# An attention block in decode: scores of one pair placed ahead of the value products of the pair in front of it

## The chip, the cores and the metric

The kernel runs on one core of one Trainium2 chip. The metric is the time of one execution on the device in microseconds (us), and for a kernel the median of several such runs. One further execution is recorded by the hardware profiler; from it come the profile and the trace. The engines are PE (matrix products), PEld (its weight loads), DVE (vector), ACT (scalar and activation functions), POOL and SP (SyncE, which here issues all the loads). L12 is line 12 of the kernel.

## The reference, cut to what matters

```python
# x: 2 rows (batch b) of 512; 32 query heads, 8 key/value heads of 128; the last W = 4096 positions
mod = silu(c) @ w_mod                                  # six vectors sa, ca, ga, sb, cb, gb per row
h = layernorm(x) * (1 + ca) + sa
q = h @ wq                                             # 32 heads of 128
scores = q . k_cache[b, head // 4, -4096:] * 128**-0.5
p = softmax(scores)
o = p . v_cache[b, head // 4, -4096:]
x = x + ga * (o @ wo)
h = layernorm(x) * (1 + cb) + sb
x = x + gb * (silu(h @ w1) @ w2)                       # w1 is 512 x 1792, w2 is 1792 x 512
```

Everything is float32. The data are read once: 16 key blocks and 16 value blocks of 2.10 MB each (8 heads, 2 batch rows), and beside them w_mod (6.3 MB), wq and wo (8.4 MB each), w1 and w2 (3.7 MB each), 97.5 MB in all.

## The kernel before, in words

**Loads.** All large loads go through one ring of 8 tiles of 2 MB in SBUF (`ring`, `RING = 8`) and are issued by SP in the order of the program: four of w_mod, four of wq, then keys and values, four of wo (L95), three of w1 and five of w2 (L95). A load waits on SP until the tile that is eight loads back in this order has been read for the last time; every load behind it on SP's queue waits with it. `fetch(t)` (L338) issues the keys of pair t (L79) and the values of pair t-1 (L86).

**Head.** The modulation, the first layer norm and the queries are computed while the first loads run; the queries are laid out block by block in `qbd`.

**The loop over pairs.** A pair is a key head with a batch row; there are 16 (`seq`, `NP`). For one pair t these steps are made:

- `keys(t, 0..3)` (L349): DVE transposes the key tile in four quarters into `kT` (two buffers).
- scores `s` (L425): PE, 16 products, which the trace shows as 32, since each is made in two passes. Then DVE takes the maximum of each row, `mx` (L433).
- row of maxima: PE turns `mx` into a row, `mT` (L368); DVE takes the maximum per query head, `mg` (L371), and spreads it, `mrow` (L377); PE turns it back into a column, `bp` (L385); ACT copies it to `bias` (L387).
- exponentials `pr` (L389) on ACT, with their sum in `rowsum`.
- the probabilities are brought into the layout of weights: DVE transposes to `xp` (L399) and multiplies to `zp` (L401), PE permutes to `pT` (L412), ACT copies to `ptb` (L419).
- `weighted` (L304): PE, 8 value products `o` (16 passes, L311), in two rounds over four column groups, then ACT copies the result to `ob` (L319).
- `collect` (L322): PE adds the four parts into `o_all` (L325), one bank that holds the sums of all pairs.

Iteration t of the loop (L359) makes the keys, scores and maxima of pair t, and everything behind the maxima of pair u = t-1. Nearly all of these instructions go through `inorder = tc.keep_in_program_order`, so each engine takes them in the order in which they are written. So the orders of the engines in iteration t are:

- PE: mT(u), bp(u), pT(u), o(u), s(t), o_all(u)
- DVE: keys 0 of t, mg(u), mrow(u), keys 1 of t, xp(u), zp(u), keys 2 and 3 of t, mx(t)
- ACT: bias(u), pr(u), ptb(u), ob(u)
- SP: keys of pair t+1, values of pair t

**Tail.** The sums are divided by the row sums (`on`, L476), transposed by `oq` (L479) and copied to `oTn` (L482); then the product with wo (`acc_o` L504, `ao` L513), the second layer norm, `hid` with w1 (L545), silu (L562 to L574), and the product with w2 (`acc_yw` L578, `acc_y` L588, `yo` L598). The five loads of w2 use the ring tiles that the last values and the four tiles of wo leave.

Of the kernel before, what the change touches and what calls it, by code (L numbers as in the profile page):

```python
# [8 lines left out]
F32 = mybir.dt.float32  # L9
AF = mybir.ActivationFunctionType  # L10
ALU = mybir.AluOpType
AX = mybir.AxisListType  # L12

P = 128
B, D = 2, 512
HQ, HKV, DH = 32, 8, 128
G = HQ // HKV
# [6 lines left out]
def adaln_block(  # L24
# [21 lines left out]
    nc = tc.nc  # L46
    SK = k_cache.shape[2]
    W = min(4096, max(256, SK // 4))
    SCALE = DH**-0.5
# [4 lines left out]
    id4 = head.tile([P, 32], F32, name="id4")  # L54
# [3 lines left out]
    work = ctx.enter_context(tc.tile_pool(name="work", bufs=2))  # L58
    once = ctx.enter_context(tc.tile_pool(name="once", bufs=1))
# [3 lines left out]
    def const(shape, name):  # L63
        return consts.tile(shape, F32, name=name)

    def bank(tag, name):
        return (psum1 if tag in "CO" else psum).tile([P, 512], F32, tag=tag, name=name)
# [9 lines left out]
    def load_k(b, h):  # L77
        t = stream(f"k{h}_{b}")
        nc.sync.dma_start(  # L79
            t, k_cache[b, h, SK - W :, :].rearrange("(p n) d -> p (n d)", p=P)  # L80
        )
        return t

    def load_v(b, h):
        t = stream(f"v{h}_{b}")
        nc.sync.dma_start(  # L86
            t, v_cache[b, h, SK - W :, :].rearrange("(p n) d -> p (n d)", p=P)
        )
        return t
# [25 lines left out]
    ident = const([P, P], "ident")  # L115
# [20 lines left out]
    group = const([P, 4], "group")  # L136
# [27 lines left out]
    negscale = const([1, 1], "negscale")  # L164
# [3 lines left out]
    mrow = [const([1, P], f"mrow{i}") for i in range(2)]  # L168
    ptb = [const([P, P + 16], f"ptb{i}") for i in range(2)]
# [4 lines left out]
    qbd = [const([P, 4, B, 4, 32], f"qbd{n}") for n in range(2)]  # L174
# [3 lines left out]
    rowsum = const([P, HKV, B], "rowsum")  # L178
# [88 lines left out]
    for k in range(4):  # L267
        wv = wqt[k].rearrange("p (n s g m) -> p n g s m", n=2, s=4, g=G)
        for n in range(2):
            for g in range(G):  # L270
# [4 lines left out]
                    start=(k == 0),  # L275
                    stop=(k == 3),
# [24 lines left out]

    o_all = bank("O", "o_all")[:, : B * DH].rearrange("p (b d) -> p b d", b=B)

    def weighted(t, b, h, vt):  # L304


        pt = ptb[t % 2]
        o_ps = bank("D", f"o{t}")
        for n in range(8):
            c = n % 4  # L310
            inorder(nc.tensor.matmul(  # L311
                o_ps[32 * c : 32 * c + 32, :],
                pt[:, 16 * n : 16 * n + 32],
                vt[:, 512 * n : 512 * n + 512],
                start=(n < 4),
                stop=(n >= 4),
            ))
        o_sb = once.tile([P, 4 * DH], F32, tag="wide", name=f"ob{t}")
        inorder(nc.scalar.copy(o_sb, o_ps))  # L319
        return o_sb  # L320

    def collect(t, b, h, o_sb):  # L322

        for m in range(4):
            inorder(nc.tensor.matmul(  # L325
                o_all[32 * m : 32 * m + 32, b, :],
                selh[:, m, HQ - G - G * h : 2 * HQ - G - G * h],
                o_sb[:, m * DH : (m + 1) * DH],
                start=(t == 0),
                stop=(t == NP - 1),  # L330
                skip_group_check=True,
            ))

    seq = [(h, b) for h in range(HKV) for b in range(B)]
    NP = len(seq)
    kt, vt, wot, kT = {}, {}, [], {}

    def fetch(t):  # L338

        if t < NP:  # L340
            kt[t] = load_k(seq[t][1], seq[t][0])
        if t > 0:
            vt[t - 1] = load_v(seq[t - 1][1], seq[t - 1][0])

    def keys(t, n4):

        if n4 == 0:
            kT[t] = ktp.tile([P, 4, 32, 32], F32, tag="kT", name=f"kT{t}")
        inorder(nc.vector.transpose(  # L349
            kT[t][:, :, 8 * n4 : 8 * n4 + 8, :].rearrange("p j n k -> p n j k"),  # L350
            kt[t][:, n4 * 1024 : (n4 + 1) * 1024].rearrange("p (n j r) -> p n j r", j=4, r=32),
        ))

    inorder = tc.keep_in_program_order
    fetch(0)
    s_ps, mx = {}, {}
    for t in range(NP + 1):  # L359
        last, now = t > 0, t < NP  # L360
        if now:
            fetch(t + 1)
            keys(t, 0)
        if last:
            u = t - 1
            h, b = seq[u]
            mT = bank("B", f"mT{u}")
            inorder(nc.tensor.matmul(mT[0:1, :P], mx[u], ident, start=True, stop=True))  # L368
            m = mrow[u % 2]
            mg = work.tile([1, G], F32, tag="mg", name=f"mg{u}")  # L370
            inorder(nc.vector.tensor_reduce(  # L371
                mg,
                mT[0:1, :P].rearrange("o (c i g) -> o g c i", c=4, g=G)[:, :, :, 0:4],
                axis=AX.XY,
                op=ALU.max,
            ))
            inorder(nc.vector.tensor_copy(  # L377
                m.rearrange("o (c i g) -> o c i g", c=4, g=G)[:, :, 0:4, :],
                mg[:, None, None, :].to_broadcast([1, 4, 4, G]),
            ))  # L380
        if now:
            keys(t, 1)
        if last:
            bp = bank("B", f"bp{u}")
            inorder(nc.tensor.matmul(bp[:, 0:1], m, negscale, start=True, stop=True))  # L385
            bias = work.tile([P, 1], F32, tag="bias", name=f"bias{u}")
            inorder(nc.scalar.copy(bias, bp[:, 0:1]))  # L387
            pr = once.tile([P, 8, 32], F32, tag="pr", name=f"pr{u}")
            inorder(nc.scalar.activation(  # L389
                pr.rearrange("p s k -> p (s k)"),  # L390
                s_ps[u],
                AF.Exp,
                bias=bias,
                scale=SCALE,
                accum_out=rowsum[:, h, b : b + 1],
            ))

            xp = once.tile([P, 8, 32], F32, tag="xp", name=f"xp{u}")
            inorder(nc.vector.transpose(xp, pr))  # L399
            zp = once.tile([P, 4, 8, 16], F32, tag="zp", name=f"zp{u}")  # L400
            inorder(nc.vector.tensor_mul(  # L401
                zp,
                xp[:, None, :, 0:16].to_broadcast([P, 4, 8, 16]),
                group[:, :, None, None].to_broadcast([P, 4, 8, 16]),
            ))
        if now:
            keys(t, 2)
            keys(t, 3)
        if last:
            tp = bank("C", f"pT{u}")[:, :P]  # L410
            for i in range(4):
                inorder(nc.tensor.matmul(  # L412
                    tp[32 * i : 32 * i + 32, :],
                    id4,
                    zp.rearrange("p c s x -> p (c s) x")[:, :, 4 * i : 4 * i + 4],
                    start=True,
                    stop=True,
                ))
            inorder(nc.scalar.copy(ptb[u % 2][:, :P], tp))  # L419
            o_sb = weighted(u, b, h, vt[u])  # L420
        if now:
            s_ps[t] = bank("A", f"s{t}")[:, :256]
            for j in range(4):
                for cc in range(4):
                    inorder(nc.tensor.matmul(  # L425
                        s_ps[t][32 * cc : 32 * cc + 32, :],
                        qbd[seq[t][0] // 4][:, seq[t][0] % 4, seq[t][1], j, :],
                        kT[t][:, j, 8 * cc : 8 * cc + 8, :],
                        start=(j == 0),
                        stop=(j == 3),  # L430
                    ))
            mx[t] = work.tile([P, 1], F32, tag="mx", name=f"mx{t}")
            inorder(nc.vector.tensor_reduce(mx[t], s_ps[t], axis=AX.X, op=ALU.max))  # L433
        if last:
            collect(u, b, h, o_sb)

    gaT, sbT, cbT = turned(ga, "gaT"), turned(sb, "sbT"), turned(cb1, "cbT")
    nc.vector.tensor_copy(hT[:, :, 1:32:16], sbT[:, :, 0:32:16])
# [24 lines left out]
    for b in range(B):  # L463
        for m in range(4):
# [4 lines left out]
                start=True,  # L469
                stop=True,  # L470
# [31 lines left out]
    for q in range(24):  # L502
        g = q % 4
# [4 lines left out]
            start=(q < 4),  # L508
            stop=(q >= 20),
        )  # L510
    for q in range(24, 32):
        for g in range(4):
# [4 lines left out]
                start=(q == 24),  # L517
                stop=(q == 31),
# [24 lines left out]
    for k in range(4):  # L543
        for g in range(4):
# [4 lines left out]
                start=(k == 0),  # L549
                stop=(k == 3),  # L550
# [25 lines left out]
    for tt in range(WIDE):  # L576
        g = tt % 4
# [4 lines left out]
            start=(tt < 4),  # L582
            stop=(tt >= WIDE - 4),
        )
    y = bank("D", "acc_y")[:, :P]
    for tt in range(WIDE, T2):
        for g in range(4):
# [4 lines left out]
                start=(tt == WIDE),  # L592
                stop=(tt == T2 - 1),
# [35 lines left out]
```

## Time and profile before

| | |
|---|---|
| median of 3 runs | 255.24 us (252.54 to 255.28) |
| time of the profiled execution | 254.44 us |
| its span, first to last instruction | 252.7 us |
| mean granted PE clock | 0.797 of full speed |
| PE busy | 153.7 us (61%) |
| DVE busy | 119.3 us (47%) |
| ACT busy | 35.5 us (14%) |
| loads | 97.5 MB, on average 386 GB/s over the span |
| value products o, one pass | 945 ns mean, 256 of them |
| scores s, one pass | 411 ns mean, 512 of them |
| transposes of keys, a quarter | 1224 ns mean, 64 of them |

Busy shares are averages over the head, the loop (46 to 222 us) and the tail. Passes on PE overlap, so their mean durations do not add up to its busy time. In the profile's slices the span is cut into 40 equal parts of 6.3 us; a digit is the busy share of a slice in tenths, and 9 is 90% or more. The chain that ended last is followed back from the last instruction; each of its lines gives the start, the duration and the work, and in time between them an engine takes over from another.

### The profile page before, as it was taken

What the parts mean: (1) busy time and instruction counts of PE and PEld (TensorE: products, weight loads), DVE (VectorE), ACT (ScalarE), POOL (GpSimd) and SP (SyncE); (2) the same over time, 40 slices, a digit from 0 to 9 for tenths busy, and PEclk for the clock granted to TensorE, in tenths of its full rate; (3) what the DMA queues carried; (4) which work ended last, traced back from release to release, by engine and by line L of the source; (5) the groups of instructions that cost most, each with busy time, mean ns of one, the idle gap of its engine ahead of it and who ended that gap; (6) DMA issues with size and microseconds to landing.
All of it is one profiled execution on the core that took longest, in us unless ns stands there. A gap on an engine that the chain in (4) does not pass through costs nothing.

```text
span 252.7 us, 3508 instructions
## 1 busy us (share of the span) xinstructions
PE 153.7 (61%) x1476; PEld 55.6 (22%) x1476; DVE 119.3 (47%) x212; ACT 35.5 (14%) x96; POOL 9.3 (4%) x30
## 2 busy tenths in 40 slices
PE   0294736555484764845749385583754849679754
PEld 0221001121231222212223121221212313232412
DVE  0703004845649457485463837549476490210230
ACT  2200000112211111112111101211012110100320
POOL 9300001000000000000000000000000000000000
PEclk9997597675978979779575977978879786657979
DMA  7999999999999999999999999999999999953800
GB/s 261 428 434 425 436 425 431 440 420 431 433 428 438 418 431 441 420 438 425 431 436 420 438 424 433 431 428 433 429 431 428 427 428 433 398 204 122 293 2 1
DMA packets 7607, 97.75 MB, mean 387 GB/s; under 512 B 920, under 2 KB 936, under 8 KB 1576
## 3 DMA queue, kind: packets, MB, share of 16 engines
q1 hardware_dynamic: 7592, 97.54, 91.5%
q8 instruction: 11, 0.18, 0.3%
q14 instruction: 4, 0.03, 0.0%
HBM read 97.53 MB, written 0.00 MB: 386 GB/s over the span
## 4 chain that ended last, share of the span: by engine, by line
PE 49%; DVE 23%; DMA 15%; ACT 8%; issue 4%; SPq 0%; DVEq 0%; ACTq 0%
PE o L311 20%; PE s L425 13%; DMA wq<-in_A_wq_dram 12%; DVE kT L349 9%; DVE zp L401 4%; PE pT L412 4%; ACT pr L389 4%; DVE xp L399 3%; PE acc_o L504 3%; DVE mx L433 3%; DMA wm<-in_w_mod_dram 2%; PE bp L385 2%; ACT ptb L419 2%; PE q L271 1%; PE acc_yw L578 1%
## 5 line engine op out<-in xcount | busy, mean ns | idle before, releaser
L349 DVE STREAM_TRANSPOSE kT<-k 128x1024 f32<-128x1024 f32 x64 | 77.0, 1224 | 0.0
L311 PE MATMUL o<-v,ptb 128*32 128x512 f32 x256 | 51.3, 945 | 6.0 <-ACT ptb L419 6.0
L425 PE MATMUL s<-kT,qbd 128*32 128x256 f32 x512 | 36.8, 411 | 2.5 <-DVE kT L349 2.3
L433 DVE TENSOR_REDUCE mx<-s 128x1 f32<-128x256 f32 x16 | 6.8, 425 | 62.8 <-PE s L425 62.8
L412 PE MATMUL pT<-zp,id 128*32 128x128 f32 x128 | 10.1, 403 | 33.8 <-DVE zp L401 33.6
L425 PEld LDWEIGHTS s<-kT,qbd 128*32 128x32 f32 x512 | 17.3, 121 | 30.7 <-issue 17.7
L271 PE MATMUL q<-wq,hq_T 128*32 128x512 f32 x64 | 12.8, 943 | 10.0 <-DMA wq<-in_A_wq_dram 10.0
L311 PEld LDWEIGHTS o<-v,ptb 128*32 128x32 f32 x256 | 9.5, 158 | 34.0 <-issue 21.0
L319 ACT COPY ob<-o 128x512 f32<-128x512 f32 x16 | 9.4, 587 | 53.4 <-PE o L311 53.4
L385 PE MATMUL bp<-negscale,mrow 1*128 1x1 f32 x32 | 6.0, 256 | 16.7 <-DVE mrow L377 16.7
L387 ACT COPY bias<-bp 128x1 f32<-128x1 f32 x16 | 2.5, 159 | 63.6 <-PE bp L385 63.6
L401 DVE TENSOR_TENSOR zp<-xp,group 128x512 f32<-128x512 f32 x16 | 11.1, 692 | 0.5
L412 PEld LDWEIGHTS pT<-zp,id 128*32 128x32 f32 x128 | 3.6, 135 | 34.7 <-issue 34.5
L280 DVE STREAM_TRANSPOSE qT<-q 128x512 f32<-128x512 f32 x2 | 1.4, 716 | 20.1 <-PE q L271 20.1
L368 PE MATMUL mT<-ident,mx 128*1 128x128 f32 x32 | 6.1, 271 | 5.6 <-DVE mx L433 5.6
L385 PEld LDWEIGHTS bp<-negscale,mrow 1*128 1x128 f32 x32 | 4.7, 182 | 21.4 <-DVE mrow L377 21.4
L399 DVE STREAM_TRANSPOSE xp<-pr 128x256 f32<-128x256 f32 x16 | 7.1, 445 | 4.3 <-ACT pr L389 2.9
L419 ACT COPY ptb<-pT 128x128 f32<-128x128 f32 x16 | 4.3, 266 | 32.5 <-PE pT L412 32.5
L389 ACT ACTIVATE pr<-s,bias 128x256 f32<-128x256 f32 x16 | 7.6, 474 | 0.7 <-ACT bias L387 0.2
L504 PE MATMUL acc_o<-wo,oTn 128*32 128x512 f32 x48 | 6.9, 736 | 0.4 <-DVE oTn L482 0.4
L325 PE MATMUL o_all<-ob,selh 128*32 128x128 f32 x128 | 6.5, 282 | 0.7 <-ACT ob L319 0.7
L271 PEld LDWEIGHTS q<-wq,hq_T 128*32 128x32 f32 x64 | 2.3, 146 | 19.8 <-DMA wq<-in_A_wq_dram 11.0
(126 smaller groups left out, 90.0 us busy)
## 6 DMA issues: line engine op xcount, KB each, us to landing
k<-in_A_k_cache_dram SPq DMA_DIRECT2D x16, 2048.0 KB, 24.5
v<-in_A_v_cache_dram SPq DMA_DIRECT2D x16, 2048.0 KB, 27.7
wq<-in_A_wq_dram SPq DMA_DIRECT2D x4, 2048.0 KB
wo<-in_A_wo_dram SPq DMA_DIRECT2D x4, 2048.0 KB, 17.6
wm<-in_w_mod_dram SPq DMA_DIRECT2D x4, 1536.0 KB, 10.1
w<-in_B_w_dram SPq DMA_DIRECT2D x2, 1024.0 KB, 4.8
w<-in_B_w_dram SPq DMA_DIRECT2D x1, 1792.0 KB
w<-in_B_w_dram SPq DMA_DIRECT2D x2, 896.0 KB
```

Of the source, the lines that this page charges most:

```text
L271: nc.tensor.matmul(q_ps[n][32 * g : 32 * g + 32, :], hq_T[:, k, :], wv[:, n, g], start=(k == 0), stop=(k == 3),)
L311: inorder(nc.tensor.matmul(o_ps[32 * c : 32 * c + 32, :], pt[:, 16 * n : 16 * n + 32], vt[:, 512 * n : 512 * n + 512], start=(n < 4), stop ...
L319: inorder(nc.scalar.copy(o_sb, o_ps))
L349: inorder(nc.vector.transpose(kT[t][:, :, 8 * n4 : 8 * n4 + 8, :].rearrange("p j n k -> p n j k"), kt[t][:, n4 * 1024 : (n4 + 1) * 1024].r ...
L385: inorder(nc.tensor.matmul(bp[:, 0:1], m, negscale, start=True, stop=True))
L389: inorder(nc.scalar.activation(pr.rearrange("p s k -> p (s k)"), s_ps[u], AF.Exp, bias=bias, scale=SCALE, accum_out=rowsum[:, h, b : b + 1],))
L399: inorder(nc.vector.transpose(xp, pr))
L401: inorder(nc.vector.tensor_mul(zp, xp[:, None, :, 0:16].to_broadcast([P, 4, 8, 16]), group[:, :, None, None].to_broadcast([P, 4, 8, 16]),))
L412: inorder(nc.tensor.matmul(tp[32 * i : 32 * i + 32, :], id4, zp.rearrange("p c s x -> p (c s) x")[:, :, 4 * i : 4 * i + 4], start=True, st ...
L425: inorder(nc.tensor.matmul(s_ps[t][32 * cc : 32 * cc + 32, :], qbd[seq[t][0] // 4][:, seq[t][0] % 4, seq[t][1], j, :], kT[t][:, j, 8 * cc ...
L433: inorder(nc.vector.tensor_reduce(mx[t], s_ps[t], axis=AX.X, op=ALU.max))
L504: nc.tensor.matmul(acc[32 * g : 32 * g + 32, :], oTn[:, q, :], wot[q // 8][:, q % 8, :], start=(q < 4), stop=(q >= 20),)
```

## The change

The same instructions are issued; their order and the grouping in the source change. The bodies of the old loop become functions (`scores`, `maxima`, `maxrow`, `exponentials`, `turn`, `permute`), with the instructions and operands that they had. `weighted` takes an argument `part` and issues four of its eight value products at each call, the copy to `ob` with the second. What moves:

- the transposes of keys: quarters 0 and 1 of t, then mg(u) and mrow(u), then quarters 2 and 3, and xp(u) and zp(u) only behind them;
- the scores of t: ahead of pT(u) and o(u);
- `collect`: one iteration later, behind the scores of t; the last one behind the loop;
- mT(t): from the head of the next iteration to between the two halves of o(u).

The orders of the engines in iteration t become:

- PE: bp(u), s(t), o_all(u-1), pT(u), half of o(u), mT(t), other half of o(u)
- DVE: keys 0 and 1 of t, mg(u), mrow(u), keys 2 and 3 of t, xp(u), zp(u), mx(t)
- ACT: bias(u), pr(u), ptb(u), ob(u)
- SP: keys of pair t+1, values of pair t

The diff, cut to the value products and the loop:

```diff
-    def weighted(t, b, h, vt):
...
-        for n in range(8):
-            c = n % 4
+    def weighted(t, vt, part):
+        if part == 0:
+            o_ps[t] = bank("D", f"o{t}")
+        for c in range(4):
+            n = 4 * part + c
             inorder(nc.tensor.matmul(
...
-                start=(n < 4),
-                stop=(n >= 4),
+                start=(part == 0),
+                stop=(part == 1),
             ))
-        o_sb = once.tile([P, 4 * DH], F32, tag="wide", name=f"ob{t}")
-        inorder(nc.scalar.copy(o_sb, o_ps))
-        return o_sb
+        if part == 1:
+            sb_ = once.tile([P, 4 * DH], F32, tag="wide", name=f"ob{t}")
+            inorder(nc.scalar.copy(sb_, o_ps[t]))
+            return sb_
...
     for t in range(NP + 1):
-        last, now = t > 0, t < NP
+        u, last, now = t - 1, t > 0, t < NP
         if now:
             fetch(t + 1)
             keys(t, 0)
-        if last:
...
-            inorder(nc.tensor.matmul(mT[0:1, :P], mx[u], ident, start=True, stop=True))
...
-        if now:
             keys(t, 1)
         if last:
...
-            inorder(nc.vector.transpose(xp, pr))
...
+            maxrow(u)
+            exponentials(u)
         if now:
             keys(t, 2)
             keys(t, 3)
         if last:
...
-            o_sb = weighted(u, b, h, vt[u])
+            zp = turn(u)
         if now:
...
-            inorder(nc.vector.tensor_reduce(mx[t], s_ps[t], axis=AX.X, op=ALU.max))
+            scores(t)
+        if t > 1:
+            collect(u - 1, seq[u - 1][1], seq[u - 1][0], o_sb[u - 1])
+        if now:
+            maxima(t)
         if last:
-            collect(u, b, h, o_sb)
+            permute(u, zp)
+            weighted(u, vt[u], 0)
+        if now:
+            inorder(nc.tensor.matmul(mT[t][0:1, :P], mx[t], ident, start=True, stop=True))
+        if last:
+            o_sb[u] = weighted(u, vt[u], 1)
+    collect(NP - 1, seq[NP - 1][1], seq[NP - 1][0], o_sb[NP - 1])
```

More of the change, by code (lines that the diff above doesn't have):

```diff
@@ L302, in adaln_block @@
     o_all = bank("O", "o_all")[:, : B * DH].rearrange("p (b d) -> p b d", b=B)
-    def weighted(t, b, h, vt):
-        pt = ptb[t % 2]
-        o_ps = bank("D", f"o{t}")
-        for n in range(8):
-            c = n % 4
+    o_ps = {}
+    def weighted(t, vt, part):
[3 more added lines that the diff above has]
+            n = 4 * part + c
             inorder(nc.tensor.matmul(
-                o_ps[32 * c : 32 * c + 32, :],
-                pt[:, 16 * n : 16 * n + 32],
+                o_ps[t][32 * c : 32 * c + 32, :],
+                ptb[t % 2][:, 16 * n : 16 * n + 32],
                 vt[:, 512 * n : 512 * n + 512],
-                start=(n < 4),
-                stop=(n >= 4),
-            ))
-        o_sb = once.tile([P, 4 * DH], F32, tag="wide", name=f"ob{t}")
-        inorder(nc.scalar.copy(o_sb, o_ps))
-        return o_sb
+                start=(part == 0),
+                stop=(part == 1),
+            ))
+        if part == 1:
+            sb_ = once.tile([P, 4 * DH], F32, tag="wide", name=f"ob{t}")
+            inorder(nc.scalar.copy(sb_, o_ps[t]))
+            return sb_
     def collect(t, b, h, o_sb):
@@ L356, in adaln_block, with scores @@
     inorder = tc.keep_in_program_order
+    s_ps, mx, mT, pr, o_sb = {}, {}, {}, {}, {}
+    def scores(t):
+        h, b = seq[t]
+        s_ps[t] = bank("A", f"s{t}")[:, :256]
+        for j in range(4):
+            for cc in range(4):
+                inorder(nc.tensor.matmul(
+                    s_ps[t][32 * cc : 32 * cc + 32, :],
+                    qbd[h // 4][:, h % 4, b, j, :],
+                    kT[t][:, j, 8 * cc : 8 * cc + 8, :],
+                    start=(j == 0),
+                    stop=(j == 3),
+                ))
@@ new lines, in maxima, with maxrow @@
+    def maxima(t):
+        mx[t] = work.tile([P, 1], F32, tag="mx", name=f"mx{t}")
+        inorder(nc.vector.tensor_reduce(mx[t], s_ps[t], axis=AX.X, op=ALU.max))
+        mT[t] = bank("B", f"mT{t}")
+    def maxrow(t):
+        m = mrow[t % 2]
+        mg = work.tile([1, G], F32, tag="mg", name=f"mg{t}")
+        inorder(nc.vector.tensor_reduce(
+            mg,
+            mT[t][0:1, :P].rearrange("o (c i g) -> o g c i", c=4, g=G)[:, :, :, 0:4],
+            axis=AX.XY,
+            op=ALU.max,
+        ))
+        inorder(nc.vector.tensor_copy(
+            m.rearrange("o (c i g) -> o c i g", c=4, g=G)[:, :, 0:4, :],
+            mg[:, None, None, :].to_broadcast([1, 4, 4, G]),
+        ))
@@ new lines, in exponentials @@
+    def exponentials(t):
+        h, b = seq[t]
+        bp = bank("B", f"bp{t}")
+        inorder(nc.tensor.matmul(bp[:, 0:1], mrow[t % 2], negscale, start=True, stop=True))
+        bias = work.tile([P, 1], F32, tag="bias", name=f"bias{t}")
+        inorder(nc.scalar.copy(bias, bp[:, 0:1]))
+        pr[t] = once.tile([P, 8, 32], F32, tag="pr", name=f"pr{t}")
+        inorder(nc.scalar.activation(
+            pr[t].rearrange("p s k -> p (s k)"),
+            s_ps[t],
+            AF.Exp,
+            bias=bias,
+            scale=SCALE,
+            accum_out=rowsum[:, h, b : b + 1],
+        ))
@@ new lines, in turn, with permute @@
+    def turn(t):
+        xp = once.tile([P, 8, 32], F32, tag="xp", name=f"xp{t}")
+        inorder(nc.vector.transpose(xp, pr[t]))
+        zp = once.tile([P, 4, 8, 16], F32, tag="zp", name=f"zp{t}")
+        inorder(nc.vector.tensor_mul(
+            zp,
+            xp[:, None, :, 0:16].to_broadcast([P, 4, 8, 16]),
+            group[:, :, None, None].to_broadcast([P, 4, 8, 16]),
+        ))
+        return zp
+    def permute(t, zp):
+        tp = bank("C", f"pT{t}")[:, :P]
+        for i in range(4):
+            inorder(nc.tensor.matmul(
+                tp[32 * i : 32 * i + 32, :],
+                id4,
+                zp.rearrange("p c s x -> p (c s) x")[:, :, 4 * i : 4 * i + 4],
+                start=True,
+                stop=True,
+            ))
+        inorder(nc.scalar.copy(ptb[t % 2][:, :P], tp))
@@ L357, in adaln_block @@
     fetch(0)
-    s_ps, mx = {}, {}
     for t in range(NP + 1):
-        last, now = t > 0, t < NP
+        u, last, now = t - 1, t > 0, t < NP
         if now:
@@ L363, in adaln_block @@
             keys(t, 0)
-        if last:
-            u = t - 1
-            h, b = seq[u]
-            mT = bank("B", f"mT{u}")
-            inorder(nc.tensor.matmul(mT[0:1, :P], mx[u], ident, start=True, stop=True))
[L369 to L380, printed above, removed]
-        if now:
             keys(t, 1)
         if last:
[L384 to L405, printed above, removed]
+            maxrow(u)
+            exponentials(u)
         if now:
@@ L409, in adaln_block @@
         if last:
[L410 to L419, printed above, removed]
-            o_sb = weighted(u, b, h, vt[u])
-        if now:
[L422 to L433, printed above, removed]
-        if last:
-            collect(u, b, h, o_sb)
+            zp = turn(u)
+        if now:
+            scores(t)
[3 more added lines that the diff above has]
+            maxima(t)
+        if last:
+            permute(u, zp)
[5 more added lines that the diff above has]
+    collect(NP - 1, seq[NP - 1][1], seq[NP - 1][0], o_sb[NP - 1])
     gaT, sbT, cbT = turned(ga, "gaT"), turned(sb, "sbT"), turned(cb1, "cbT")
```

## The prediction, made before the changed kernel ran

> **What bounds the kernel now.** I read the slices of the page first, then the chain of work that ended last within one pair, then the busy times by stretch, then the landings of the loads, then SyncE's own waits.
>
> ```profile
> PE   0294736555484764845749385583754849679754
> DVE  0703004845649457485463837549476490210230
> DMA  7999999999999999999999999999999999953800
> ```
>
> No compute engine is full in the loop (slices 8 to 33), but the DMA engines are at 9 from the start to about 214 us. The chain of one pair, in between, holds compute alone, and nothing in it waits for a load:
>
> ```profile
> 86.18 1.15 DVE kT L349
> ...
> 87.70 0.39 PE bp L385 x2
> ...
> 88.30 0.57 ACT pr L389 x2
> ...
> 88.90 0.46 DVE xp L399
> ...
> 89.38 0.70 DVE zp L401
> ...
> 90.22 0.69 PE pT L412 x8
> ...
> 90.93 0.28 ACT ptb L419
> ...
> 91.25 2.97 PE o L311 x16
> 94.21 1.78 PE s L425 x32
> ...
> 96.02 0.42 DVE mx L433
> 96.44 1.15 DVE kT L349
> ```
>
> One pair takes 10.26 us, in which PE and DVE mostly take turns. Both things hold at once because the loads are ahead of the compute:
>
> ```profile
> 38.74:195.00 156.26, 96.66 (x940) 35.14 (x940) 94.62 (x137) 23.55 (x73) 0.95 (x4) 0.79 1.01 430
> ...
> 233.40:237.80 4.40, 2.72 (x79) 2.11 (x71) 1.46 (x9) 1.87 (x2) 0.00 (x0) 1.00 0.97 347
> 244.00:247.40 3.40, 3.40 (x24) 1.07 (x28) 0.00 (x0) 0.00 (x0) 0.00 (x0) 0.56 0.00 0
> ```
>
> A stretch's row ends with granted clock, DMA share and GB/s: 430 GB/s at a full share, so a 2.10 MB tile needs 4.88 us and a pair (keys and values) 9.75. The last two rows are of the tail and are used below. Two landings, of the only key load issued between 61 and 62 us and of the only wo load issued between 198 and 199:
>
> ```profile
> DMA to landing us min/median/max: 25.9/25.9/25.9
> ```
>
> ```profile
> wo<-in_A_wo_dram SPq DMA_DIRECT2D x1, 2048.0 KB, 17.0
> ```
>
> The first, issued at 61.38, is pair 5, the tenth tile behind wq: landed at 87.3. The second, issued at 198.19, is the 36th tile: landed at 215.2. wq ended at 38.74 (chain), so tile n lands at 38.74 + 4.90n: (87.3 - 38.74)/10 = 4.86, (215.2 - 38.74)/36 = 4.90. Keys of pair 15 (n = 30) land at 185.7, its values (n = 32) at 195.5. The kernel transposes those keys at 202.2 to 208.4 and starts o of pair 15 at 218.6: data wait 16 to 23 us for compute. SyncE's waits (91.2 us of k loads behind kT) say the same: ring slots come free late.
>
> **The change part by part.** No compute instruction and no DMA is added or removed; fetch stays where it was in the program. S is the end of scores s(t), u the pair in front.
>
> 1. *Scores ahead of values.* PE's order is now s(t), o_all(u-1), pT(u), half of o(u), mT(t), other half, bp(t). After S, PE runs o_all 0.2 to 0.39, pT 0.69, ACT's ptb 0.28 with 0.06 of hand-over, o half 1.49, mT 0.39: S+3.3. Second half: S+4.8.
> 2. *Keys in halves.* DVE runs mx to S+0.45 and k0, k1 (2 x 1.18) to S+2.8. mg waits for mT: S+3.3, a new wait of 0.5 with mrow, k2, k3 queued behind it. mg and mrow take 0.4: S+3.7; k2, k3: S+6.1. The next s follows (1.78): S' = S+7.9, against 10.26.
> 3. *The softmax behind it.* bp waits for PE to S+4.8, then 0.39, bias 0.2 (ACT is in ob until S+5.4), exponential with its accumulator read 0.66: S+6.3. xp and zp (0.46 + 0.70) end at S+7.5, beside s(t), before mx needs DVE. Cost: nothing; if that cover goes, mx, mT and the next mg come later by up to 1.16.
> 4. *The added waits.* mT sits between two halves of an accumulation and waits for mx, ready at S+0.45, long before its turn. No trace shows a matmul to another bank inside such a group. Lower bound nothing, if it fits into PE's weight-load gaps (a gain is excluded: it is one more matmul in a dense stretch); upper 0.73, its 0.39 and the 0.34 that PE waited ahead of it in the old order. I take 0.39, its own row.
> 5. *collect one turn later, one collect behind the loop*: 0.39 a pair beside DVE's zp and mx; the last one is on the path as it was.
>
> So the free loop is 7.9 us. At half clock (the rows with clock 0.50 to 0.56: o 3.64, s 2.79, o_all 0.39) it is 0.39 + 0.69 + 0.34 + 1.82 + 0.39 + 0.4 + 2.36 + 2.79 = 9.2. Either way below the 9.75 of the loads. Saved alone, (10.26 - 7.9) x 15 would be 35 us; but the first s ends at 53.5 and the loop catches the loads at about pair 5 (53.9 + 5 x 7.9 = 93, keys 5 at 87). From there a new thing is late: k(t) itself. DVE waits for it with mrow(u) queued behind, so the softmax of u starts when the keys of t land. That costs the loop nothing while loads set the pace. Loads stay fed: values of u land 4.9 us behind keys t and are released 12.7 us behind them (185.7 to 198.4 in the walk below), and their slot's next load has its turn 39 us behind them, four pairs on. SyncE's queue, in order, therefore never holds a due load back.
>
> **The end, worked out.** Keys 15 land at 185.7; keys and maxima 5.1: 190.8; s at half clock (PE's bursts begin at 0.50 in the rows, 90.2 to 92.4) 2.79: 193.6; o_all, pT, ptb 1.4, half 1.5, mT 0.4, half 1.5: 198.4; bp, bias, exponential 1.5: 199.9; xp, zp 1.2, pT, ptb 1.0: 202.1; o 3.64: 205.7, against 222.26 now. From there to acc_o is 4.48 in this trace (222.26 to 226.74): 210.2. acc_o 6.92, ao done 9.04 behind its start: 219.2 (wo landed by 215.2). hid starts 2.02 later: 221.3.
>
> Now loads decide. Behind wo come w1 (3.67 MB) and w2 (3.67 MB), eight pieces. Their slots: w2's first needs o(15) (205.7), the others acc_o and ao (213 to 219), all before their turn in the queue, which is busy to the end. w1 at 420 GB/s (the stretch 210 to 215 has 421): 215.2 + 8.7 = 223.9. First w2 piece 2.5: 226.4. The remaining 2.62 MB at the 347 of the stretch shown above, whose pieces they are: 7.55, 233.95. Last matmuls 0.2: yo at 234.2. The compute path beside it: last quarter of hid at half clock 1.7 behind 223.9: 225.6; hid to acc_yw 2.54 (241.46 to 244.00): 228.1; to yo 5.29 (249.29 - 244.00): 233.4. So loads win by 0.8. yo to the end 3.41 (252.7 - 249.29): span 237.6. The profiled execution took 254.44, its span 252.7: 1.74 around it. Sum 239.3, which is 15.1 less than 254.44; the median of the runs, 255.24, lies 0.8 above that.
>
> Unknown terms: the rest of w2 at 430 instead of 347 takes 1.45 off, but the compute path then decides, so 0.8 in all; the stream at 434 (the row of 75.9 to 86.2) instead of the 428 of 4.90 us a tile takes 176.5 x 6/434 = 2.4 off; both together 236.1. The upper ends are the rivals'.
>
> **The rivals.**
> - *Loop slower than its parts*, 10.0 us a pair (hand-overs that I do not see, 2.1 us over my walk): first mx ends at 53.9, + 150, + 12.1 from mx to the end of the last o (193.6 to 205.7) = 216.0, + 30.44 as now from there to the end, + 1.74: 248.2; less about 1 where the waits on wo are gone: 247. For it: 116.9 to 140 shows pairs of 11 to 12 us. Against: those are the half clock, which I priced.
> - *Half clock to the end*, as PE's bursts are split by waits: o halves +0.64, so the last o ends at 206.3; acc_o from 210.8, 12 groups of 0.855 (its first four take that): 221.1; ao 4.6, the step to hid 2.0, hid 7.4: 235.1; 2.5, last stage 7.6: 245.2; + 3.41 + 1.74 = 250.3. Against: acc_o is a burst of 7 us, and the clock is 1.00 from 230.2 on. For it: behind only 2.5 us of idle (241.5 to 244.0) the row of 244.0 shows 0.56. [...]
> - *The end of the stream gives it back* (no change): the eight small pieces each pay a start of their own. The lone first w2 piece took 4.8 us for 2.44 of bytes; 8 x 2.1 to 2.36 on top of 239.3: 256 to 258, so 257. Against: the four last pieces took 8.2 us together where bytes need 6.1, one start of 2.1 for all. [...]
> - *Slower: the stream slows* when transposes follow each landing at once. It decides at 394 GB/s (95.1 MB behind 8 us, landed by 249). At the mean of the whole span, 386: 82.8 MB behind 38.74 end at 253.3, + 0.2 + 3.41 + 1.74: 258.7. Against: 425 to 435 in every stretch, with DVE from 46% to 64% busy. [...]
>
> **How the numbers follow.** Chances: load-bound 239.3: 0.74 (own range 235.5 to 242); slow loop 247: 0.10; half clock 250.3: 0.05; given back 257: 0.05; slower stream 258.7: 0.06 (half of it at 381 GB/s or less, where it passes 260.3). The range takes in the first two: 235.5 to 247. A measurement of this kernel can tell about 2%: 250.1 and 260.3 against 255.24. Faster: 0.74 + 0.10 = 0.84; within: half clock, given back and half of the slower stream, 0.13; slower: its other half, 0.03.
>
> **What would show it.** Loop period 9.75 to 9.8 from pair 5 on with kT waiting for k loads; SyncE's k waits on kT shrinking; s starting behind the last kT, mT between halves of o without idle; last o near 206; DMA share 9 up to about 233; hid waiting for w1. Wrong, if pairs stay at 10 us with no load waited for, or if DMA shows holes before 225.

## The result, and the profile after

The changed kernel takes 238.74 us (median of 4 runs, 237.98 to 239.76), the kernel before 254.87 us (4 runs, the three shown above among them): a ratio of 0.939, 95% interval 0.932 to 0.946. The forecast was 239.3. The profiled execution took 237.98 with a span of 236.2, against 254.44 and 252.7.

First the slices of the page of the changed kernel (each is now 5.9 us long):

```profile
PE   0193864395978777596876869659768696694843
DVE  0614000658688947658476594764946742102130
DMA  6999999999999999999999999999999999999990
```

The compute rows look like before; the DMA row has lost its hole: it is full until about 230 us. Before, the digit 9 ended at 221 us (the prediction reads 214), and the three slices behind moved 204, 122 and 293 GB/s. No more bytes are moved, and they move no faster (430 GB/s between 38.75 and 195 us in both kernels). They end earlier because ring tiles come free in time: SyncE issues the eight loads of w1 and w2 between 186.1 and 217.7 us, where it took from 200.1 to 236.1.

The chain that ended last (start, duration, work) now reads:

```profile
53.94 2.28 DVE kT L352 x2
...
67.84 29.17 DMA k<-in_A_k_cache_dram
...
97.03 2.37 DVE kT L352 x2
...
102.02 34.19 DMA k<-in_A_k_cache_dram
...
180.15 34.96 DMA wo<-in_A_wo_dram
...
215.17 16.53 DMA w<-in_B_w_dram
...
231.75 1.06 PE acc_y L616 x24
```

From the landing of wq (38.75 us) up to 68 us it is compute, as before. From there on the steps are mostly loads. Keys and wo take 29 to 35 us from issue to landing; at 4.9 us a tile that is a queue of six or seven tiles. 78% of the chain is DMA, where it was 15%. One pair of that stretch in the timeline (start, duration, engine, line; in brackets the idle time ahead and what ended it):

```profile
136.23 2.37 DVE L352 STREAM_TRANSPOSE kT<-k 128x1024 f32<-128x1024 f32 x2 [0.91 <-DMA k<-in_A_k_cache_dram]
...
138.53 0.17 DVE L384 TENSOR_REDUCE mg<-mT 1x4 f32<-1x64 f32 x1
...
138.84 2.35 DVE L352 STREAM_TRANSPOSE kT<-k 128x1024 f32<-128x1024 f32 x2
138.97 0.38 PE L398 MATMUL bp<-negscale,mrow 1*128 1x1 f32 x2 [1.20 <-DVE mrow L390]
...
141.25 3.19 PE L368 MATMUL s<-kT,qbd 128*32 128x256 f32 x25 [0.51 <-DVE kT L352]
...
144.87 0.42 DVE L378 TENSOR_REDUCE mx<-s 128x1 f32<-128x256 f32 x1 [2.62 <-PE s L368]
...
145.93 2.37 DVE L352 STREAM_TRANSPOSE kT<-k 128x1024 f32<-128x1024 f32 x2 [0.64 <-DMA k<-in_A_k_cache_dram]
```

DVE starts on the keys when they land, and waits for the next ones. Two things are to be seen. The row of mg has no bracket, so the row of maxima was already there. And DVE waits for keys, 0.91 and 0.64 us in these two pairs and 16.9 us in 11 pairs in all. The scores, which took 1.78 us on the chain of before, take 3.6 behind the last quarter in this pair.

### The profile page after: what moved, and what is told of

Read it like the earlier page. It is cut to its first block, busy times and chain, and to the rows that moved or that the text cites. A ratio compares the mean times of both kernels' runs of the same rounds, so it can differ in the third digit from the quotient of the medians.

```text
span 236.2 us, 3508 instructions
## 1 busy us (share of the span) xinstructions
PE 160.8 (68%) x1476; PEld 61.9 (26%) x1476; DVE 118.3 (50%) x212; ACT 35.2 (15%) x96; POOL 9.3 (4%) x30
## 4 chain that ended last, share of the span: by engine, by line
DMA 78%; DVE 14%; PE 5%; SPq 1%; issue 0%; ACT 0%; DVEq 0%
DMA k<-in_A_k_cache_dram 41%; DMA wo<-in_A_wo_dram 15%; DMA wq<-in_A_wq_dram 13%; DVE kT L352 12%; DMA w<-in_B_w_dram 7%; DMA wm<-in_w_mod_dram 3%; PE s L368 3%; PE q L271 2%; SPq L74 1%; PE acc_y L616 0%; DVE qbd L294 0%; DVE mrow L390 0%; DVE mx L378 0%; DVE qT L280 0%; ACT qbd L294 0%
## 5 line engine op out<-in xcount | busy, mean ns | idle before, releaser
L352 DVE STREAM_TRANSPOSE kT<-k 128x1024 f32<-128x1024 f32 x64 | 75.4, 1215 | 17.0 <-DMA k<-in_A_k_cache_dram 16.9
L368 PE MATMUL s<-kT,qbd 128*32 128x256 f32 x512 | 69.2, 512 | 9.0 <-DVE kT L352 8.2
L313 PE MATMUL o<-v,ptb 128*32 128x512 f32 x256 | 35.4, 630 | 5.7 <-ACT ptb L433 5.7
L368 PEld LDWEIGHTS s<-kT,qbd 128*32 128x32 f32 x512 | 23.4, 139 | 46.0 <-DVE kT L352 29.6
L328 PE MATMUL o_all<-ob,selh 128*32 128x128 f32 x128 | 12.6, 295 | 1.1 <-ACT ob L322 0.7
L426 PE MATMUL pT<-zp,id 128*32 128x128 f32 x128 | 13.2, 298 | 0.2 <-DVE zp L416 0.2
L313 PEld LDWEIGHTS o<-v,ptb 128*32 128x32 f32 x256 | 7.8, 111 | 11.7 <-ACT ptb L433 10.4
L328 PEld LDWEIGHTS o_all<-ob,selh 128*32 128x32 f32 x128 | 7.5, 124 | 4.4 <-ACT ob L322 2.3
L426 PEld LDWEIGHTS pT<-zp,id 128*32 128x32 f32 x128 | 7.7, 123 | 0.9 <-issue 0.5
L414 DVE STREAM_TRANSPOSE xp<-pr 128x256 f32<-128x256 f32 x16 | 6.4, 397 | 2.2 <-ACT pr L402 2.2
## 6 DMA issues: line engine op xcount, KB each, us to landing
wm<-in_w_mod_dram SPq DMA_DIRECT2D x4, 1536.0 KB, 10.3
```

Source lines behind the costliest of these rows:

```text
L313: inorder(nc.tensor.matmul(o_ps[t][32 * c : 32 * c + 32, :], ptb[t % 2][:, 16 * n : 16 * n + 32], vt[:, 512 * n : 512 * n + 512], start=(p ...
L328: inorder(nc.tensor.matmul(o_all[32 * m : 32 * m + 32, b, :], selh[:, m, HQ - G - G * h : 2 * HQ - G - G * h], o_sb[:, m * DH : (m + 1) * DH],
L352: inorder(nc.vector.transpose(kT[t][:, :, 8 * n4 : 8 * n4 + 8, :].rearrange("p j n k -> p n j k"), kt[t][:, n4 * 1024 : (n4 + 1) * 1024].r ...
L368: inorder(nc.tensor.matmul(s_ps[t][32 * cc : 32 * cc + 32, :], qbd[h // 4][:, h % 4, b, j, :], kT[t][:, j, 8 * cc : 8 * cc + 8, :], start= ...
L426: inorder(nc.tensor.matmul(tp[32 * i : 32 * i + 32, :], id4, zp.rearrange("p c s x -> p (c s) x")[:, :, 4 * i : 4 * i + 4], start=True, st ...
```

## The experiments

Theory: the changed loop has a chain shorter than the loads of a pair need, so loads set the pace and the end. Rivals: one part of the change alone does it; the chain still sets the pace; the half clock of PE costs time (the profile shows stretches at half of full speed, as 141.25 to 144.44 us of the changed kernel at a granted clock of 0.50). Ratios are to the kernel before, run beside each; that of the change itself is 0.939.

### Each part alone

Keys only: on the kernel before, DVE takes quarters 0 and 1, row of maxima, quarters 2 and 3, xp, zp.

```diff
             keys(t, 0)
+            keys(t, 1)
         if last:
...
-        if now:
-            keys(t, 1)
...
         if now:
             keys(t, 2)
             keys(t, 3)
+        if last:
+            xp = once.tile([P, 8, 32], F32, tag="xp", name=f"xp{u}")
+            inorder(nc.vector.transpose(xp, pr))
...
```

> The kernel before, with only the order on DVE changed: quarters 0 and 1 of the keys, row of maxima, quarters 2 and 3, and only then xp and zp; PE's order is that of before. Theory (the loop is one chain of waits; halves alone put all four quarters on it, since o waits for zp and s for o): 2.28 + 0.35 + 2.3 + 0.46 + 0.84 + 0.69 + 0.3 + 2.97 + 1.78 + 0.44 = 12.4 us a pair instead of 10.3, so some 32 us slower than before, 283 to 292. Rival (fewer hand-overs on DVE are what helps): faster than before, below 252.

Measured 298.29 us, ratio 1.176 (1.170 to 1.182). Part of its chain, one pair:

```profile
163.24 2.28 DVE kT L349 x2
...
165.83 2.28 DVE kT L349 x2
168.11 0.34 DVE xp L402
...
168.47 0.70 DVE zp L404
...
169.31 0.69 PE pT L411 x8
...
170.33 3.64 PE o L311 x16
```

All four quarters stand in the chain, then o, then s. The steps are those expected; a pair takes 13.65 us instead of 12.4, since o runs at 3.64 instead of 2.97 and s longer as well, at a lower clock (0.764 over the span, where the kernel before had 0.797). The theory's sign and mechanism hold; its size was 1.2 us a pair too small, and the time lies above the expected range.

Scores only: the changed kernel with the quarters where they stood before.

```diff
             keys(t, 0)
-            keys(t, 1)
         if last:
             maxrow(u)
+        if now:
+            keys(t, 1)
+        if last:
             exponentials(u)
+            zp = turn(u)
         if now:
             keys(t, 2)
             keys(t, 3)
-        if last:
-            zp = turn(u)
-        if now:
             scores(t)
```

> The changed kernel, with the keys of before on DVE: quarter 0, row of maxima, quarter 1, xp, zp, quarters 2 and 3, then the scores. Theory (scores may run ahead only when the last quarter is early; now the softmax of the pair in front stands before it): from the end of s, mg at 2.7, mrow 3.0, quarter 1 4.2, pr 4.25, xp and zp 5.5, quarters 2 and 3 7.9, s at 9.8 to 10.9 by its clock; above the 9.8 of the loads, so most of the gain is gone: 245 to 262. Rival (the order on PE alone brings the gain): as the changed kernel, 239.

Measured 263.09 us, ratio 1.038 (1.033 to 1.044): slower than the kernel before, by 1 us outside the range. Its chain in one pair:

```profile
120.65 1.06 PE o L313 x8
...
121.81 1.03 PE o L313 x5
...
122.86 0.28 ACT ob L322
...
123.54 0.57 ACT pr L402 x2
...
124.62 0.69 DVE zp L416
125.31 2.29 DVE kT L352 x2
...
127.64 2.99 PE s L368 x25
```

The softmax of the pair in front now stands ahead of quarters 2 and 3 and with them of s: both halves of o, ob, pr, zp, keys, s in one line, 11.4 us a pair. So neither part brings anything; each alone costs, 44 and 9 us, and both together save 16. Rival one falls for these two parts. The later place of `collect` was in scores only and in the change, and was not tried alone.

### Half of the loads left out

```diff
-            kt[t] = load_k(seq[t][1], seq[t][0])
+            kt[t] = kt[t - 1] if t % 2 else load_k(seq[t][1], seq[t][0])
...
-            vt[t - 1] = load_v(seq[t - 1][1], seq[t - 1][0])
+            vt[t - 1] = load_v(seq[t - 1][1], seq[t - 1][0]) if t % 2 else vt[t - 2]
```

> The changed kernel with half of the key and value loads left out (each odd pair works on the keys and values of the pair before it, so the output is another one); all instructions of the other engines remain. Theory (loads set the pace of the changed loop): the loop runs free at 7.3 us a pair, the last o ends near 174, and with 30 us of tail and 1.8 around the span it takes 206 (203 to 213). Rival (the loop's chain sets the pace already): pairs stay near 9.8 and the time near 236 to 239.

> The kernel before, with half of the key and value loads left out (each odd pair works on the keys and values of the pair before it, so the output is another one). Theory (its loop is a chain of its own instructions, and loads were ahead of it): no change, 252 to 256, pairs still 10.3 us. Rival (loads held back the kernel before as well): clearly faster, toward the 206 of the changed kernel with half of the loads.

Measured: changed kernel with half 206.59 us, ratio 0.815 (0.811 to 0.819); kernel before with half 254.89, ratio 1.003 (0.999 to 1.007). One pair of each, by its row of the stretches (busy times of PE, PEld, DVE, ACT, POOL, then clock, DMA share, GB/s), the changed kernel first:

```profile
99.20:106.50 7.30, 6.03 (x69) 2.63 (x68) 6.28 (x11) 1.51 (x5) 0.00 (x0) 1.00 0.68 249
```

```profile
128.80:139.20 10.40, 6.43 (x69) 2.41 (x70) 6.47 (x10) 1.58 (x5) 0.00 (x0) 0.84 0.39 135
```

Without half of the loads the changed loop runs at 7.30 us a pair in all but its first pair, and the kernel before gains nothing, with its DMA engines idle for 60% of that stretch. Loads set the pace of the changed kernel and not of the one before: shown from both sides. That the loads left out might have slowed the engines as well is ruled out by the changed kernel itself: its early pairs take the same 7.30 us while the loads run at their full rate.

```profile
62.90:70.20 7.30, 6.01 (x68) 2.63 (x68) 6.28 (x11) 1.48 (x5) 0.00 (x0) 1.00 1.00 426
```

### The row of maxima between the halves

```diff
-        if now:
-            inorder(nc.tensor.matmul(mT[t][0:1, :P], mx[t], ident, start=True, stop=True))
         if last:
             o_sb[u] = weighted(u, vt[u], 1)
+        if now:
+            inorder(nc.tensor.matmul(mT[t][0:1, :P], mx[t], ident, start=True, stop=True))
```

> The changed kernel, with the row of maxima turned behind both halves of o instead of between them. Theory (loads set the pace; the chain of the loop grows by some 0.75 us, to about 8.1 where it runs free and below 9.8 in any case): no change, 238 to 240. Rival (the loop's own chain sets the pace): 16 x 0.75 = 12 us slower, 251.

> The changed kernel with the row of maxima turned behind both halves of o, and half of the key and value loads left out (another output), so that the loop runs free. Theory (mT between the halves is worth 0.7 us of the loop's chain, hidden while loads set the pace): pairs at 8.0 instead of 7.3 us, some 217 instead of 206.6. Rival (its place never mattered): 206 to 207.

Measured 239.06 us with all loads, ratio 0.944 (0.938 to 0.949), not to be told from the changed kernel; with half of the loads 208.15 us (one run) where 217 was expected and 206.59 is the value without the edit. From the timeline of the latter:

```profile
99.64 2.36 DVE L352 STREAM_TRANSPOSE kT<-k 128x1024 f32<-128x1024 f32 x2
...
101.79 0.38 PE L462 MATMUL mT<-ident,mx 128*1 128x128 f32 x2
...
102.21 0.21 DVE L384 TENSOR_REDUCE mg<-mT 1x4 f32<-1x64 f32 x1 [0.21 <-PE mT L462]
```

mg waits 0.21 us and a pair takes 7.63 instead of 7.30. So the middle place of mT is worth 0.33 us a pair, hidden here, and I had it at 0.75: o takes 1.92 us in one piece there, not the 2.97 of before, so that even its end comes about when DVE is done with the second quarter of the keys. The total shows less than 15 times 0.33: the last o ends 4.4 us later (178.1 instead of 173.7), and the tail behind it was 3.1 us shorter (28.3 instead of 31.4); the granted clock was 0.921 over the span instead of 0.908, and why the tail was shorter is open. By its total the run lies nearer to the rival, and the reading rests on the pairs.

### How much cover the loop has

Work repeated on DVE, in the chain and without effect on the result: mx twice (0.43 us; first diff), quarter 2 twice (1.18; the first added line of the second diff), quarters 2 and 3 twice (2.36; both lines).

```diff
-        inorder(nc.vector.tensor_reduce(mx[t], s_ps[t], axis=AX.X, op=ALU.max))
+        for _ in range(2):
+            inorder(nc.vector.tensor_reduce(mx[t], s_ps[t], axis=AX.X, op=ALU.max))
```

```diff
             keys(t, 2)
+            keys(t, 2)
             keys(t, 3)
+            keys(t, 3)
```

> The changed kernel, with the maximum mx taken twice (0.43 us more on the loop's chain in each pair, same result). Theory (the loop waits for keys, in the trace 0.6 to 1.5 us a pair): the wait shrinks by 0.43 and the time stays, 238 to 240. Rival (no cover): 16 x 0.43 = 7 us slower, 245.6.

> The changed kernel, with quarter 2 of the keys transposed twice (1.18 us more on the loop's chain). Theory: from landing to the next free DVE the chain is 9.06 where s runs at half clock (3.6 behind the last quarter) and would be 7.3 at full clock; with 1.18 more, 10.2 or 8.5 against the 9.8 of the loads. At half clock throughout it would take 55 + 15 x 10.2 + 9.4 + 30.2 + 1.8 = 249; at full clock 239. I expect something between, 239 to 246, since a pair without a wait closes PE's gaps and raises its clock. Rival (no cover): 16 x 1.18 = 19 us slower, 257.6.

> The changed kernel, with quarters 2 and 3 of the keys each transposed twice (2.36 us more on the loop's chain). Theory: 11.4 us a pair at half clock, 9.7 at full clock, against the 9.8 of the loads: 240 if the clock stays up, 269 if it stays at half; the loop no longer waits for keys in any pair at half clock, so I expect 250 to 269. Rival (the slack is the whole 2.5 us between 7.3 and 9.8, whatever the clock): 239 to 242.

Measured: 239.01 us (ratio 0.940, 0.934 to 0.946), 247.20 (0.972, 0.967 to 0.977), 268.57 (1.056, 1.050 to 1.061). The wait of DVE for keys in the changed kernel (us, times, longest):

```profile
DVE kT L352 <- DMA k<-in_A_k_cache_dram: 16.9, 11, 2.4
```

and with mx taken twice:

```profile
DVE kT L352 <- DMA k<-in_A_k_cache_dram: 7.6, 8, 2.1
```

The first extra 0.43 us comes out of this wait and costs nothing, the next 0.75 costs 8 us, and 2.36 cost 30. The 2.5 us between 7.3 and 9.8 are not there as cover; I expected 239 to 246 for 1.18 and it lay just above, near the 249 that half clock gives. Its pairs settle at 10.24 us, which less 1.18 is the 9.06 of the theory: no wait of DVE for keys is in this run's list of waits, and yet 25 passes of the scores took 3.20 us, as at the granted clock of 0.50 in the changed kernel (3.19), and DVE waited 2.4 to 2.6 us for them in every steady pair; so the hope that the clock would rise with the wait gone failed.

### The clock

Two products of 128 x 384 with an identity behind bp (three with 2.36 us of extra work), written to columns that nothing reads, so that PE has work while DVE transposes:

```diff
         inorder(nc.tensor.matmul(bp[:, 0:1], mrow[t % 2], negscale, start=True, stop=True))
+        for _ in range(2):
+            inorder(nc.tensor.matmul(bp[:, P:], ident, quad[:, 0:3, :], start=True, stop=True))
```

> The changed kernel with quarter 2 transposed twice (as the run before with 1.18 us more), and two products of 128 x 384 with an identity behind bp on PE, in the stretch where PE otherwise waits for the keys; they write columns of bp's bank that nobody reads. Theory (the scores run at half clock since PE idles ahead of them, and this is what eats the slack): with the gap filled the clock stays up, s takes 2.0 instead of 3.6 behind the last quarter, the chain is 8.5 to 8.9 and the loop waits for loads again: 238 to 241. Rival (the clock has another cause, or the slack is small for another reason): 247 as without them, or more, since two more products stand ahead of s.

> The same with quarters 2 and 3 transposed twice (2.36 us more) and three such products. Theory: chain 9.7 to 9.9 at full clock, about the pace of the loads: 239 to 244. Rival: 268.6 as without them.

> The changed kernel with the two products behind bp and nothing else. Theory (loads set the pace): the time stays, 237.5 to 239.5, and only the waits for keys grow to some 2 us a pair; the last pair ends about 1 us earlier, where the tail waits for wo in any case. Rival (the half clock costs time in the changed kernel too): faster by up to 16 x 1.6 = 25 us.

Measured: 238.39 us (ratio 0.943, 0.939 to 0.948) with 1.18 us of extra work, 247.59 (0.972, 0.964 to 0.981) with 2.36, 238.48 (0.942, 0.939 to 0.946) with no extra work on DVE. A pair with 1.18 us of extra work, without the products:

```profile
135.40:145.60 10.20, 7.65 (x69) 3.25 (x68) 7.49 (x11) 1.51 (x5) 0.00 (x0) 0.83 1.00 430
```

and with them, over 10 us:

```profile
139.00:149.00 10.00, 7.73 (x75) 3.60 (x75) 7.92 (x11) 1.57 (x5) 0.00 (x0) 1.00 1.00 426
```

The clock goes from 0.83 to 1.00, s behind the last quarter (25 passes) from 3.20 to 1.70 us, the pair from 10.2 to 8.57 in the first half of the loop, where loads are still ahead, and the time is that of the changed kernel again: more work on PE, less time. With 2.36 us the chain became 9.86 us a pair, as expected (9.7 to 9.9), but my 239 to 244 was wrong: at 9.86 us a pair against the 9.75 of the loads the loop never made up the lead that these have at 46 us, and its last mx came at 204.6 instead of 193.1. On the changed kernel itself the products change nothing that can be told (238.48 us at a granted clock of 0.869 in the profiled run, where 238.74 and 0.848 stand without them): loads decide. Rival three falls there. The mean rate over the whole span is 414 GB/s already, against 430 in the full stretches, so little seems left to take without moving fewer bytes.

## Why the prediction was right, step by step

- *What bounded the kernel before* (a chain of compute, with the data waiting): shown by the run of before with half of the loads.
- *Landings.* Keys of pair 15 forecast at 185.7; in the trace DVE starts on them at 184.95, when they land; last wo 215.2, in the trace 215.1. The rate of the stream was the same with both orders of the compute (430 GB/s between 38.75 and 195 us), and the rival with a slower stream fell.
- *The loop alone*: forecast 7.9 us a pair at full clock, measured 7.30, so the rival of the slow loop (10.0) fell; 9.2 at half clock, measured 9.06 from landing to the end of mx in the pair shown (136.23 to 145.29), and 7.4 to 9.1 in the eleven pairs that waited, as more or less of s fell into half clock. That 9.2 came so close to the worst pairs is luck: the prediction had the first half of o at half clock (1.82), mg waiting for it, and s at 2.79; in the trace half of o takes 1.06, mg waits for nothing, and s takes 3.6 behind the last quarter. The path was another one too: the prediction ran it through PE (o_all, pT, half of o, mT) to mg, and in the trace it runs through DVE (mx, then the keys) to s, with o beside it. The catch-up came at pair 5, as forecast: the first pairs took 9.00, 7.30, 7.30, 7.45 and the next ones 8.0 to 11.5, on average 9.9. The mis-sized term is step 1, o in two halves of 1.49: they took 1.07 and 1.02. PE comes out of its pause with the scores now. In the pair shown 25 of their 32 passes had a granted clock of 0.50 (141.25 to 144.44 us) and o had 1.00 (135.65 to 137.77); in the trace of before o had 0.63 (91.25 to 94.20) and s 1.00 (94.21 to 96.00). A pass of s went from 411 to 512 ns on average and one of o from 945 to 630:

```profile
L368 PE MATMUL s<-kT,qbd 128*32 128x256 f32 x512 | 69.2, 512 | 9.0 <-DVE kT L352 8.2
...
L313 PE MATMUL o<-v,ptb 128*32 128x512 f32 x256 | 35.4, 630 | 5.7 <-ACT ptb L433 5.7
```

- *The added waits.* The wait of mg for mT, put at 0.5, is nothing in the steady loop: mg starts right behind the second quarter in the pair shown above. In the last pair, where no keys stand ahead of it, it is 1.63. The softmax behind the keys cost nothing, as forecast.
- *The drain.* Last o forecast to end at 205.7, ended at 202.9; acc_o forecast from 210.2, began at 206.3. Same cause, and oq took 1.08 us at a granted clock of 1.00 instead of 1.94 at 0.50. Neither mattered, since ao waited for the last wo (1.91 us of idle on PE ahead of it) and the last part of hid for w1.
- *The end.* w1 and w2 were to end at 233.95 with 347 GB/s for the last four pieces. They ended at about 232.3: from the landing of the last wo to that of the last piece of w2, 7.34 MB in 17.2 us or 427 GB/s. That term was mis-sized by 1.6 us. In the trace of before these pieces were issued 1.7 to 2.1 us apart (230.3 to 235.8), and here they stood in a full queue, so 347 is not the price of small pieces. Why they were slower there is open: the DMA share of that stretch was 0.97, so the engines did not stand idle. The 8.2 us that the prediction read for them leave out part of the issue and of the landings; the first was issued at 230.3, and the third landed at 240.7. yo began at 232.83 instead of 234.2, and the span is 236.2 instead of 237.6; the 1.74 around the span were 1.78. The sum of 239.3 was built for the profiled execution, which took 237.98; that it is only 0.6 from the median is in part luck, since the median of the four runs lies 0.8 above the profiled one.
- *A start for each piece.* The rival read 2.1 to 2.36 us for a start from the trace of before; eight of them would be 17 to 19 us. Queued behind one another the eight pieces show none: 7.34 MB at 430 GB/s are 17.1 of the 17.2 us, and that rival fell.
- *The clock.* The longest idle stretch of PE in the pair shown above is the 1.20 us ahead of bp (in the whole loop it is 2.68 us), and the 25 passes of the scores behind the last quarter ran at half clock: granted clock 0.50 between 141.25 and 144.44 us; the row of the whole pair, below, has 0.82. In the 3.45 us ahead of them (137.80 to 141.25) PE was busy for 1.55 us. With two products more in that stretch, in the run with 1.18 us of extra work, the granted clock was 1.00 instead of 0.83. It was not so in every pair: in two of the eleven that waited for keys s ran at full clock (25 passes in 1.70 us at a granted clock of 1.00, from 150.95 and from 170.39 us). The rival of half clock to the end fell in the tail, where its price lay: acc_o took 6.91 us where the rival had 10.3, and the granted clock was 1.00 from 224.75 us to yo. In the loop half clock cost nothing, since even 9.06 us a pair still fits under the loads, by 0.7 us.

```profile
136.23:145.93 9.70, 7.42 (x72) 3.17 (x67) 6.37 (x9) 1.58 (x5) 0.00 (x0) 0.82 0.99 424
```

So the mechanism (loads set the pace from pair 5 on, and they set the end) was right, and the margin was smaller than the 7.9 against 9.75 on which I mainly argued: in the pairs that wait the loop needs up to 9.1 against 9.75. The prediction had priced that state too, at 9.2.

## What to carry to other kernels

Before pricing a reorder, ask what comes next as the bound, and price the end by that: here 15 x 3 us of loop were freed and 16 us came out, and the 16 could be read from the landings in the trace of before. Parts of a reorder can each be a loss and together a gain, since a step moved early helps only if nothing late stands ahead of it on the other engine's queue; trying parts one by one would have thrown this one away. Cover has to be measured in the state the loop settles in: here the scores fell into half clock (0.50 in the pair shown) while the loop waited for loads, at worst 9.06 us a pair instead of 7.30, and its cover was nearer to 0.7 us than to 2.5.

## What the runs showed of the hardware that was not expected

- Throwaway products made a kernel faster: with 1.18 us of extra DVE work in each pair, two products more on PE took it from a ratio of 0.972 (0.967 to 0.977) to 0.943 (0.939 to 0.948), through the clock (0.83 to 1.00).
- With the order the half clock moved from one group of products to another, with no change to either instruction: before, the row of 90.2 to 92.4 us, where o starts, has a granted clock of 0.50; in the changed kernel it is the row of 141.25 to 144.44, where s runs. A pass of o went from 945 to 630 ns, a pass of s from 411 to 512.
- Eight loads of 0.26 to 1.8 MB, queued behind full ones, ran at 427 GB/s from landing to landing, about the rate of the 2.1 MB tiles (430); the last four had shown 347 GB/s in the trace of before.
